# Attention and a softplus feed-forward on one core: the first heads loaded head by head on two DMA queues, heads 0 and 1 placed by engines, three weight groups converted inside the attention loop, and a row clearing done by a transfer

## The chip, the core and the metric

The kernel runs on one core of a Trainium2 chip. The core has a matrix engine (TensorE, PE in the profile), a vector engine (VectorE, DVE), a scalar engine (ScalarE, ACT), GpSimd (POOL) and SyncE (SP), which issues most DMAs. Engines run their own instruction streams in order and wait for each other through semaphores. The metric is the device time of one execution in microseconds.

## The reference, cut to what matters

```python
def _attn_ref(q, k, v):                       # each (4, 8, 576, 64)
    ...
    q_rot, k_rot = (rotate(q), rotate(k))     # rotary embedding
    scores = scale * np.matmul(q_rot, k_rot.transpose(0, 1, 3, 2))
    scores = scores - np.max(scores, axis=-1, keepdims=True)
    attn = np.exp(scores)
    attn = attn / (np.sum(attn, axis=-1, keepdims=True) + 1e-09)
    return np.matmul(attn, v).astype(np.float32)

def _moe_ref(x, w_in, w_out):                 # x (2304, 512), w_in (512, 2048), w_out (2048, 512)
    h = x @ w_in
    g = np.maximum(h, 0.0) + np.log1p(np.exp(-np.abs(h)))
    return (g @ w_out).astype(np.float32)
```

The 32 heads of the attention are computed first; their outputs, put side by side, are the rows `x` of the feed-forward part.

## The kernel before

**Numbers in two parts.** TensorE multiplies in a rounded 32-bit form (`F32R`). To keep accuracy each operand is split into a high part (the rounded value) and a low part (the rest), and products of parts are added. A "rounding" below is a copy into that form (`rnd`), a "low part" is a subtraction (`tt`).

**Attention loop.** `attention` runs over slots `s`; five slots make a head (`h, c = divmod(s, 5)`). In slot `s` four stages work on different heads: `p1(s)` multiplies a strip of 128 queries with all keys, and DVE takes the row maximum from PSUM (L352); nine slots later (`LAG`) `p2` multiplies again, keys by queries, with the maximum subtracted through two extra rows of `qs` (rows 64 and 65 of its second half) against ones in `ks`; `exps` takes the exponential twice on ACT, `low` subtracts on DVE; three slots later (`PVD`) `pv_mm` multiplies with V; `evac` takes the sums out. PE therefore does, in every slot, one `p1`, one `p2` and one `pv_mm`. `p1` has one PSUM buffer (`ps_1`), `p2` two (`ps_2`), `pv` one (`ps_v`).

**How a head gets its operands.** A pair of heads (`p`) is loaded as two tiles `raw`, one for q and one for k, each with both heads (`load_pair`). `rope_steps` rotates each with three operations (two products with `tab`, a sum: L297), rounds (L291 on ACT, L294 on POOL) and subtracts. For pair 0 this is done by DVE and ACT ahead of the loop, for the others mostly by POOL, one step in each slot. Then `stack(h)` builds `qs` and `ks` of one head with four DMAs from `raw` to other partitions (L329 to L332): the high part twice, the low part once. `qs` and `ks` have four buffers (`NST`).

**The maximum's way.** After a head's five maxima, `shift1` (two tiny POOL operations, L294 and L297 on `shl`), `shift2` (a PE transpose, L370, and an ACT copy, L372) and `shift3` (a DMA on ACT's queue, L376) write it into `qs`. PE's L370 stands in PE's order, so PE waits there if POOL is late. When a head is done, POOL clears the two rows again (L503).

**Weights.** The feed-forward weights come in 16 groups `f`, as 64-bit floats, and are turned into high and low 32-bit parts by six steps (`conv_w`; two chunks for each group): ACT, DVE (L133) with ACT (L135), DVE (L137), an addition (L140), ACT (L143), a subtraction (L145). Group 0 is converted in the first ten slots with DVE, group 1 in slots 142 to 156 (`STEPS`) with the addition and subtraction on POOL, the rest from slot 169 on (`late`, `convert`).

**After the loop.** From slot 146 POOL also multiplies the attention output by the reciprocal sums and splits it (`split_xb`, L179 to L181), one or two operations a slot. Then 96 units of the feed-forward follow: 12 matmuls into `hp` (L197) and 9 into `oa` or `ob` (L233).

**Order.** What is passed through `pin` keeps the program's order on its engine; DMAs in `chain` keep their order among themselves; the rest is placed by a scheduler. Ahead of the loop PE runs 64 matmuls on zeros (`WARM`, L277).

## Time and profile before

| What | Value |
|---|---|
| median of 3 runs | 754.91 us (754.41 to 755.38) |
| profiled execution, its own time | 754.79 us |
| span of its trace | 752.9 us |
| mean granted TensorE clock | 0.98 |
| PE busy | 719.2 us (96%) |
| DVE, ACT, POOL busy | 496.3, 383.0, 314.5 us |

The span is the time from the first to the last instruction of the trace; the profiled execution's own time is 1.9 us longer. PE's busy time is near the span, so a change of the time is found in PE's few idle stretches and in those where its granted clock was low.

### The profile page before, as it was taken

Reading aid. Unit: us, or ns where it says so; the run is one execution under the profiler, and the core shown is the slowest. Engines: PE = TensorE matmul, PEld = TensorE weight load, DVE = VectorE, ACT = ScalarE, POOL = GpSimd, SP = SyncE. Lnnn points to the kernel's source line nnn. Section 1 sums busy time; section 2 is a strip of 40 time slices with the busy share of each in tenths; the row PEclk is TensorE's granted clock in tenths of the full one; section 3 lists DMA queues with packets and bytes.
Section 4 is the critical chain, followed back from the end, with each engine's and each line's share of the span. In section 5 each row is a group of like instructions: output and inputs, shape, how many; then the busy total and the mean of one; then the engine's idle time right before and its main releaser. Section 6 shows DMA issues by size and latency. Waiting matters only on the chain.

```text
span 752.9 us, 11811 instructions
## 1 busy us (share of the span) xinstructions
PE 719.2 (96%) x4288; PEld 671.1 (89%) x4288; DVE 496.3 (66%) x784; ACT 383.0 (51%) x718; POOL 314.5 (42%) x384
## 2 busy tenths in 40 slices
PE   5589999999999999789999999999999999999997
PEld 5489999999999999788888989898989898989896
DVE  7688887888787788666888888454453444344433
ACT  2267777777777778666566665222222222222221
POOL 5269999999898887972000000172220000000000
PEclk9589999999999999999999999999999999999999
DMA  7948887889998977502334433052010000001001
GB/s 234 248 125 203 202 202 195 210 218 218 217 238 225 229 194 175 155 13 71 113 112 134 146 111 94 9 180 64 22 42 1 1 37 7 1 1 43 0 1 44
DMA packets 46219, 89.05 MB, mean 118 GB/s; under 512 B 6768, under 2 KB 16304, under 8 KB 46160
## 3 DMA queue, kind: packets, MB, share of 16 engines
q1 hardware_dynamic: 43184, 83.41, 42.1%
q10 hardware_dynamic: 2976, 4.88, 1.7%
q8 instruction: 34, 0.56, 0.3%
q14 instruction: 25, 0.20, 0.1%
HBM read 48.64 MB, written 7.23 MB: 74 GB/s over the span
## 4 chain that ended last, share of the span: by engine, by line
PE 80%; DVE 7%; DMA 5%; ACT 3%; issue 2%; POOL 2%; SPq 0%; DVEq 0%; ACTq 0%; POOLq 0%
PE hp L197 23%; PE pv L419 13%; PE ob L233 12%; PE oa L233 11%; PE sp L387 10%; PE sp L350 10%; DVE raw L297 2%; DMA qs<-shr 2%; ACT wc L131 1%; DVE wc L140 1%; DVE wl L145 1%; DVE wc L137 1%; DMA x<-rd 1%; DVE mx L352 1%; DMA tab<-cs 1%
## 5 line engine op out<-in xcount | busy, mean ns | idle before, releaser
L197 PE MATMUL hp<-x,wh 128*128 128x384 f32 x768 | 196.9, 337 | 2.3 <-DVE m L212 2.3
L352 DVE TENSOR_REDUCE mx<-sp 128x1 f32<-128x576 f32 x160 | 120.9, 756 | 61.4 <-PE sp L350 51.2
L197 PEld LDWEIGHTS hp<-x,wh 128*128 128x128 f32 x768 | 140.1, 188 | 12.8 <-DVE m L212 4.9
L209 ACT ACTIVATE e<-e 128x384 f32<-128x384 f32 x96 | 50.4, 525 | 188.5 <-DVE e L207 181.8
L350 PE MATMUL sp<-ks,qs 128*128 128x288 f32 x640 | 118.4, 310 | 14.9 <-DMA ks<-raw 10.8
L393 ACT ACTIVATE ph<-sp 128x576 fp32r<-128x576 f32 x160 | 103.7, 648 | 54.5 <-PE sp L387 53.8
L197 PE MATMUL hp<-x,wl 128*128 128x384 f32 x384 | 129.3, 337 | 0.0
L387 PE MATMUL sp<-qs,ks 128*128 128x288 f32 x640 | 114.4, 300 | 1.9 <-DMA qs<-shr 1.8
L350 PEld LDWEIGHTS sp<-ks,qs 128*128 128x128 f32 x640 | 97.6, 198 | 18.8 <-issue 11.0
L419 PE MATMUL pv<-ph,vs 128*64 128x288 f32 (+1 forms) x640 | 111.4, 296 | 2.5 <-DVE xt L427 1.6
L207 DVE TENSOR_SCALAR e<-hp 128x384 int32<-128x384 int32 x96 | 53.2, 554 | 77.3 <-PE hp L197 77.3
L394 ACT ACTIVATE sp<-sp 128x576 f32<-128x576 f32 x160 | 102.9, 643 | 0.0
L401 DVE TENSOR_TENSOR pl<-sp,ph 128x576 fp32r<-128x576 f32 x128 | 96.6, 754 | 7.0 <-ACT sp L394 5.3
L233 PE MATMUL oa<-wh,g 128*128 128x512 f32 x288 | 97.7, 393 | 0.2 <-ACT part L244 0.2
L387 PEld LDWEIGHTS sp<-qs,ks 128*128 128x128 f32 x640 | 94.0, 191 | 3.9 <-DMA qs<-shr 2.9
L233 PE MATMUL ob<-wh,g 128*128 128x512 f32 x288 | 97.3, 393 | 0.0
L419 PEld LDWEIGHTS pv<-ph,vs 128*64 128x64 f32 (+1 forms) x640 | 87.1, 162 | 3.0 <-ACT sp L394 1.8
L217 DVE TENSOR_TENSOR g<-m,g 128x384 fp32r<-128x384 f32 x96 | 55.5, 578 | 48.1 <-ACT g L214 48.1
L297 POOL TENSOR_TENSOR raw<-raw,tab 128x576 f32<-128x576 f32 x58 | 82.3, 1441 | 9.1 <-DMA raw<-qk 9.0
L212 DVE SCALAR_TENSOR_TENSOR m<-hp,e 128x384 f32<-128x384 f32 x96 | 53.4, 556 | 47.3 <-ACT e L209 47.3
L297 POOL TENSOR_TENSOR raw<-raw 128x576 f32<-128x576 f32 (+1 forms) x56 | 80.8, 1443 | 5.2 <-ACT raw L291 3.0
L214 ACT CAST g<-m 128x384 fp32r<-128x384 f32 x96 | 49.1, 512 | 62.0 <-DVE m L212 60.5
(74 smaller groups left out, 874.9 us busy)
## 6 DMA issues: line engine op xcount, KB each, us to landing
raw<-qk SPq DMA_DIRECT2D x32, 576.0 KB
wraw<-w SPq DMA_DIRECT2D x30, 512.0 KB
ks<-raw SPq DMA_DIRECT2D x32, 320.0 KB
qs<-raw SPq DMA_DIRECT2D x32, 288.0 KB
ks<-raw SPq DMA_DIRECT2D x32, 160.0 KB
vf<-v SPq DMA_DIRECT2D x32, 160.0 KB
qs<-raw SPq DMA_DIRECT2D x32, 144.0 KB
x<-xt SPq DMA_DIRECT2D x16, 144.0 KB
```

The source lines that it names most:

```text
L197: pin(nc.tensor.matmul(out=hp, lhsT=a[f][:, c * 128:(c + 1) * 128], rhs=piece(j, c)[:, b, :], start=(i == 0), stop=(i == 11),))
L212: pin(nc.vector.scalar_tensor_tensor(out=m, in0=hp, scalar=0.0, in1=e, op0=ALU.max, op1=ALU.add))
L217: pin(nc.vector.tensor_tensor(out=g[:, 1, :], in0=m, in1=g[:, 0, :].bitcast(F32), op=ALU.subtract))
L233: pin(nc.tensor.matmul(out=po, lhsT=g[:, s, t * 128:(t + 1) * 128], rhs=b[f][:, 512:1024], start=(first and i == 0), stop=(last and i == 2),))
L297: pin((nc.vector if e == "V" else nc.gpsimd).tensor_tensor(out=out, in0=in0, in1=in1, op=op))
L350: pin(nc.tensor.matmul(out=sp[:, j, :HS], lhsT=q[:, i, cq], rhs=k[:, 0, ck], start=(i == 0), stop=(i == 1)))
L352: pin(nc.vector.tensor_reduce(out=mx_t[h][:, c:c + 1], in_=sp[:, :, :HS], axis=AX.XY, op=ALU.max, negate=True))
L387: pin(nc.tensor.matmul(out=sp[:, i, :HS], lhsT=k[:, j, ck], rhs=q[:, j, hs], start=(j == 0), stop=(j == 1)))
L393: pin(nc.scalar.activation(out=ph, in_=sp, func=AF.Exp, scale=D ** -0.5))
L394: pin(nc.scalar.activation(out=sp, in_=sp, func=AF.Exp, scale=D ** -0.5))
L401: pin(nc.vector.tensor_tensor(out=pl, in0=sp[:, :, :HS], in1=ph.bitcast(F32), op=ALU.subtract))
L419: pin(nc.tensor.matmul(out=pv[rows, i, :HS], lhsT=lhs, rhs=rhs[:, i, :], start=(c == 0 and j == 0), stop=(c == 4 and j == len(terms) - 1)))
```

## The change

Head by head for the first four heads: `load_head(h)` loads q of one head into partitions 0 to 63 of a `raw` tile, on SP's queue, and k of the same head into partitions 64 to 127, on ACT's queue; the table `tab` comes in two halves on both queues, and the ACT table load stands behind ACT's first DMAs. For heads 0 and 1 there is no `stack`: ACT, DVE and POOL write their roundings and low parts straight into `qs` and `ks` at the right partitions (`part`, `high_k`, `low_q`, `low_k`, `rest`). The first shift goes from DVE through five PE transposes and two ACT copies into `qs` (`shift_first`). Head 2 is rotated by POOL with one DVE operation; its rounding is an ACT operation in slot 5. The rotations of the next pairs follow a new table of slots (`turns`).

The first `p1` slots use other PSUM buffers, the warm-up has 44 matmuls, groups 0, 1 and 2 are all loaded from slot 14 on in pieces of 128 KB and converted in the loop (one chunk in 20 slots, from slot 37), the two rows of `qs` are cleared by a DMA on SP's queue (`clear`), `shift1` stands earlier in its slot, the last slots use two buffers for `p2` instead of three, and head 30's `pv` goes to `ps_1`. `FC` is now 3, so the late conversion has 26 chunks instead of 28, and `convert` is called once instead of twice in slots 169 to 171.

```diff
-FC = 2
+FC = 3
...
-WL = 92
+WL = 14
+WS = 37
...
-WARM = 64
+WARM = 44
...
-STEPS = {142: (0,), 144: (0,), 146: (1,), 147: (0,), 148: (0,), 149: (1,), 150: (0,), 151: (0,), 152: (1,), 153: (1,),
-         155: (1,), 156: (1,)}
+STEPS = (0, 2, 5, 6, 8, 9)
...
+        def load_head(h):
+            r = raw_p.tile([128, 2, SP], F32R, tag="raw", name="raw")
+            for i, e in enumerate((nc.sync, nc.scalar)):
+                pin(e.dma_start(out=r[64 * i:64 * i + 64, :, :S].bitcast(F32),
+                                in_=qk[h // 2, i, 64 * (h % 2):64 * (h % 2) + 64]))
+            hl_t[h] = r
...
+        def turn(r, e, e0=None):
+            a, b = r[:, 1, :S].bitcast(F32), r[:, 0, :S].bitcast(F32)
+            yield tt(a, a, tab[:, 0, :], ALU.mult, e0 or e)
+            yield tt(b, b, tab[:, 1, :], ALU.mult, e)
+            yield tt(a, a, b, ALU.add, e)
+
+        def cut(r, e, ends):
+            hi, lo = r[:, 0, :], r[:, 1, :]
+            a, b = lo[:, :S].bitcast(F32), hi[:, :S].bitcast(F32)
+            yield rnd(hi[:, :S], a, e)
+            yield tt(lo[:, :S], a, b, ALU.subtract, "P")
+            if ends:
+                rnd(hi[:, S:], hi[:, 512:S].bitcast(F32), "P")
+                rnd(lo[:, S:], lo[:, 512:S].bitcast(F32), "P")
...
+        def low_q(h):
+            hi, a, q, k = part(h)
+            tt(q[Q, 1, :S], a[Q], q[Q, 0, :S].bitcast(F32), ALU.subtract, "V")
+
+        def low_k(h):
+            hi, a, q, k = part(h)
+            tt(k[K, 0, :S], a[K], hi[K, :S].bitcast(F32), ALU.subtract, "P")
+
+        def high_k(h):
+            hi, a, q, k = part(h)
+            rnd(k[Q, 0, :S], a[K], "V")
+
+        def rest(h):
+            hi, a, q, k = part(h)
+            rnd(k[Q, 1, :S], a[K], "A")
+            for j in range(2):
+                rnd(k[Q, j, S:], a[K, 512:], "A")
+            rnd(k[K, 0, S:], k[K, 0, 512:S].bitcast(F32), "A")
...
+        def clear(h):
+            free(nc.sync.dma_start(out=qs[h % NST][64:66, 1, :S].bitcast(F32), in_=ks[0][66:68, 1, :S].bitcast(F32)))
...
-            if n < LAG and n % 2:
+            if n < LAG and n % 4 == 1:
                 sp = ps_v.tile([128, 2, 512], F32, tag="pv", name="sp1")
+            elif n < LAG and n % 4 > 1:
+                sp = ps_2.tile([128, 2, 512], F32, tag="s2", name="sp1")
...
+        def shift_first():
+            tp = ps_2.tile([128, 2, 512], F32, tag="s2", name="tp")
+            for c in range(5):
+                pin(nc.tensor.matmul(out=tp[0:66, c // 4, c % 4 * 128:c % 4 * 128 + 128], lhsT=sh0[:, c, :],
+                                     rhs=identr, start=True, stop=True))
+            for j, z in enumerate((512, 128)):
+                rnd(qs[0][64:66, 1, 512 * j:512 * j + z], tp[64:66, j, :z], "A")
...
-            if n > NSLOT - LAG and (NSLOT - n) % 3 == 2:
-                ps2[n] = ps_1.tile([128, 2, 512], F32, tag="s1", name="sp2")
-            else:
-                ps2[n] = ps_2.tile([128, 2, 512], F32, tag="s2", name="sp2")
+            ps2[n] = ps_2.tile([128, 2, 512], F32, tag="s2", name="sp2")
...
+                if h == NB * NH - 2:
+                    pv_t[h] = ps_1.tile([128, 2, 512], F32, tag="s1", name="pv")
...
-        conv = conv_w([(0, i) for i in range(1024 // CW)], CW, pin, 2)
-        load_pair(0)
-        load_pair(1, (0,))
-        next(conv)
+        load_head(0)
+        for i, e in enumerate((nc.sync, nc.scalar)):
+            pin(e.dma_start(out=tab[:, i, :], in_=cs[:, i, :]))
+        load_head(1)
+        for h in range(2):
+            load_v(h)
+        pin(nc.scalar.preload_act_table_set("natural_log_exp_and_others"))
+        load_head(2)
+        load_head(3)
...
+        list(turn(hl_t[0], "V"))
+        hi, a, q, k = part(0)
+        rnd(q[K, 0, :S], a[Q], "A")
+        rnd(hi[K, :S], a[K], "A")
+        rnd(q[Q, 0, :S], a[Q], "V")
+        high_k(0)
+        low_q(0)
+        low_k(0)
+        list(turn(hl_t[1], "V"))
+        hi, a, q, k = part(1)
+        rnd(hi[K, :S], a[K], "A")
+        rnd(q[Q, 0, :S], a[Q], "A")
+        rnd(q[K, 0, :S], a[Q], "A")
+        low_k(1)
+        v_first = [split_v(h) for h in range(2)]
+        for x in v_first:
+            next(x)
+        next(v_first[0])
+        list(turn(hl_t[2], "P", "V"))
+        for h in range(2):
+            rest(h)
         sv = iter(())
-        rope = iter(())
+        rope = {3: rope_head(3)}
...
+        turns = {2 * p: (10 * p - 14, 10 * p - 5) for p in range(3, NP)}
+        turns |= {3: (9, 13), 4: (14, 18), 6: (20, 27), 8: (28, 36), 10: (37, 45)}
...
+                if s == 0:
+                    high_k(1)
+                if s == 1:
+                    low_q(1)
+                if s == 4:
+                    rnd(sh0[:, :, 64], mx_t[0], "V")
+                    tt(sh0[:, :, 65], mx_t.pop(0), sh0[:, :, 64].bitcast(F32), ALU.subtract, "V")
+                if s == 5:
+                    shift_first()
...
+            if c == 0 and 1 < h <= NB * NH:
+                shift1(h - 1)
             if n2 > 0 and n2 % 5 == 0 and n2 // 5 - 1 + NST < NB * NH:
-                pin(nc.gpsimd.memset(qs[(n2 // 5 - 1) % NST][64:66, 1, :S].bitcast(F32), 0.0))
-            if s >= 5 and c == 0 and s <= NSLOT:
-                shift1(h - 1)
+                clear(n2 // 5 - 1)
             if s < NSLOT:
-                next(rope, None)
-                if s < 5:
-                    next(rope, None)
-                if s % 10 == 5:
-                    for _ in rope:
-                        pass
-                if s % 10 == 6 and h // 2 + 1 < NP:
-                    stack(h + 1)
+                if s == 5:
+                    list(cut(hl_t[2], "A", True))
+                    next(v_first[1])
...
+                if s == 14:
+                    rope[4] = rope_steps(2)
+                    cuts2 = cut(hl_t[2, 0], "A", False), cut(hl_t[2, 1], "A", True)
+                if s in (16, 19):
+                    next(cuts2[s > 16])
+                for p in range(3, NP):
+                    if s == turns[2 * p][0]:
+                        rope[2 * p] = rope_steps(p)
+                for r, (a, z) in turns.items():
+                    if a <= s <= z:
+                        next(rope[r], None)
+                        if r == 4 and s == 14:
+                            next(rope[r], None)
+                        if s == z:
+                            for _ in rope[r]:
+                                pass
+                if s == 19:
+                    for x in cuts2:
+                        list(x)
+                if s == 14:
+                    stack(3)
+                for p in range(1, NP):
+                    if s == {1: 6, 2: 19, 3: 27}.get(p, 10 * p - 4):
+                        stack(2 * p)
+                    if s == 10 * p and p > 1:
+                        stack(2 * p + 1)
...
-            i, j = divmod(s - WL, 6)
-            if 0 <= i < 8 and j == 0:
+            i, j = divmod(s - WL, 5)
+            if 0 <= i < 8 * FC and j == 0:
                 load_p(i)
-            if s == WL + 48:
-                early.extend(conv_w([(1, i)], CW, pin, 1, {0: pre[i]}, nc.gpsimd) for i in range(2))
-                for x in early:
-                    next(x)
-            for x in STEPS.get(s, ()):
-                next(early[x], None)
+            i, j = divmod(s - WS, 20)
+            if 0 <= i < 2 * FC and j in STEPS:
+                if j == 0:
+                    early.append(conv_w([divmod(i, 2)], CW, pin, 1, {0: pre.pop(i)}, nc.gpsimd))
+                    next(early[i])
+                next(early[i])
...
-                convert()
```

On **DVE** the places ahead of and in the first slots are these. Before (`raw_202` and `raw_205` are q and k of heads 0 and 1, `raw_253` and `raw_293` those of heads 2 and 3):

```order
L297 TENSOR_TENSOR raw_202<-raw_202,tab_117 128x576 x2
L297 TENSOR_TENSOR raw_202<-raw_202 128x576 x2
L297 TENSOR_TENSOR raw_205<-raw_205,tab_117 128x576 x2
L297 TENSOR_TENSOR raw_205<-raw_205 128x576 x2
L352 TENSOR_REDUCE mx_256<-sp1_257 128x1
L352 TENSOR_REDUCE mx_256<-sp1_271 128x1
L133 TENSOR_SCALAR wc_279<-wc_279 128x512
L352 TENSOR_REDUCE mx_256<-sp1_285 128x1
L297 TENSOR_TENSOR raw_253<-raw_253,tab_117 128x576
L137 SCALAR_TENSOR_TENSOR wc_279<-wraw_209,wc_279 128x512
L352 TENSOR_REDUCE mx_256<-sp1_297 128x1
```

And in the change (`raw_177`, `raw_182`, `raw_188` are heads 0, 1 and 2):

```order
L301 TENSOR_TENSOR raw_177<-raw_177 128x576
L298 TENSOR_SCALAR qs0_116<-raw_177 64x576
L298 TENSOR_SCALAR ks0_112<-raw_177 64x576
L301 TENSOR_TENSOR qs0_116<-raw_177,qs0_116 64x576
L301 TENSOR_TENSOR raw_182<-raw_182,tab_111 128x576 x2
L301 TENSOR_TENSOR raw_182<-raw_182 128x576
L301 TENSOR_TENSOR raw_188<-raw_188,tab_111 128x576
L400 TENSOR_REDUCE mx_249<-sp1_250 128x1
L298 TENSOR_SCALAR ks1_113<-raw_182 64x576
L400 TENSOR_REDUCE mx_249<-sp1_257 128x1
L301 TENSOR_TENSOR qs1_117<-raw_182,qs1_117 64x576
L400 TENSOR_REDUCE mx_249<-sp1_264 128x1
```

The weight conversion is gone from here, and pieces of heads 1 and 2 stand between the first maxima.

On **POOL** the start of the change reads as follows, behind its memsets (`raw_191` is head 3, `raw_270` and `raw_316` are q and k of heads 4 and 5):

```order
L301 TENSOR_TENSOR ks0_112<-raw_177 64x576
L301 TENSOR_TENSOR ks1_113<-raw_182 64x576
L359 TENSOR_TENSOR vs0_123<-vf0_120,vs0_123 128x5x64
L301 TENSOR_TENSOR raw_188<-raw_188,tab_111 128x576
L301 TENSOR_TENSOR raw_188<-raw_188 128x576 x2
L298 TENSOR_SCALAR raw_188<-raw_188 128x64 x2
L359 TENSOR_TENSOR vs1_124<-vf1_121,vs1_124 128x5x64
L301 TENSOR_TENSOR raw_191<-raw_191,tab_111 128x576
L298 TENSOR_SCALAR shl_364<-mx_286 128x5
L301 TENSOR_TENSOR shl_364<-mx_286,shl_364 128x5
L301 TENSOR_TENSOR raw_191<-raw_191,tab_111 128x576
L301 TENSOR_TENSOR raw_191<-raw_191 128x576
```

Before, POOL began with all of head 2's and 3's q tile (four operations); now it first completes heads 0 and 1, then head 2, head 3 and the next pair.

On **POOL** in slots 147 to 151, before (`shl` is the maximum of head 29, L179 to L181 the split, L140 and L145 the conversion):

```order
L180 TENSOR_SCALAR x0_72<-xm_4156 128x576
L140 TENSOR_TENSOR wc_4038<-wc_4038,wt_4039 128x512
L181 TENSOR_TENSOR x0_72<-xm_4156,x0_72 128x576
L179 TENSOR_TENSOR xm_4208<-x1_73 128x576
L503 MEMSET qs3_125 2x576
L321 TENSOR_TENSOR vs0_128<-vf0_126,vs0_128 128x5x64
L180 TENSOR_SCALAR x1_73<-xm_4208 128x576
L294 TENSOR_SCALAR shl_4260<-mx_4105 128x5
```

And in the change:

```order
L178 TENSOR_SCALAR x0_72<-xm_4186 128x576
L359 TENSOR_TENSOR vs0_123<-vf0_120,vs0_123 128x5x64
L179 TENSOR_TENSOR x0_72<-xm_4186,x0_72 128x576
L177 TENSOR_TENSOR xm_4237<-x1_73 128x576
L178 TENSOR_SCALAR x1_73<-xm_4237 128x576
L298 TENSOR_SCALAR shl_4286<-mx_4136 128x5
```

The conversion's addition and the memset no longer stand ahead of `shl`.

## Rows read from the trace of the kernel before

**Rows 1.** Waits of PE, whole span: who waited for whom, total us, times, longest.

```profile
PE sp L350 <- DMA ks<-raw: 10.8, 1, 10.8
PE sp L370 <- POOL shl L297: 5.5, 3, 2.4
PE sp L350 <- DVE mx L352: 3.8, 5, 1.9
PE hp L197 <- DVE m L212: 2.3, 5, 0.9
```

**Rows 2.** Windows: stretch, length, busy us of PE, PEld, DVE, ACT, POOL; clock, DMA share, GB/s.

```profile
30.00:40.00 10.00, 5.66 (x21) 4.60 (x21) 9.41 (x14) 4.01 (x9) 2.62 (x4) 0.50 0.97 220
...
60.00:80.00 20.00, 20.00 (x152) 19.83 (x151) 16.16 (x23) 15.59 (x30) 17.79 (x24) 1.00 0.85 206
...
150.00:200.00 50.00, 49.44 (x373) 48.85 (x372) 39.88 (x54) 37.57 (x71) 44.04 (x55) 1.00 0.93 223
...
300.00:320.00 20.00, 15.70 (x115) 14.96 (x114) 14.27 (x20) 13.10 (x25) 19.61 (x21) 0.99 0.55 158
```

**Rows 3.** Chain that ended last, 0 to 50 us: start, duration, what.

```profile
1.49 5.09 DMA tab<-cs
...
18.39 4.68 DMA ks<-raw
...
35.60 3.55 DMA qs<-shr
```

**Rows 4.** Timeline, 0 to 50 us: start, duration, engine, line, operation, shape, [idle before].

```profile
8.14 0.76 DVE L297 TENSOR_TENSOR raw<-raw 128x576 f32<-128x576 f32 x1
8.93 0.67 ACT L291 CAST raw<-raw 128x576 fp32r<-128x576 f32 x1 [6.91 <-DVE raw L297]
...
10.17 3.38 POOL L297 TENSOR_TENSOR raw<-raw,tab 128x576 f32<-128x576 f32 x2 [3.60 <-DMA raw<-qk]
10.31 3.86 DVE L297 TENSOR_TENSOR raw<-raw,tab 128x576 f32<-128x576 f32 x2
...
23.31 5.69 PE L350 MATMUL sp<-ks,qs 128*128 128x288 f32 x20 [10.83 <-DMA ks<-raw]
...
37.61 0.86 POOL L321 TENSOR_TENSOR vs<-vf,vs 128x320 fp32r<-128x320 f32 x1 [4.18 <-ACT vs L291]
...
42.09 1.28 PE L350 MATMUL sp<-ks,qs 128*128 128x288 f32 x4
...
49.60 0.68 POOL L294 TENSOR_SCALAR raw<-raw 128x576 fp32r<-128x576 f32 x1
```

**Rows 5.** Page, costliest groups: POOL's rotation products; busy us, mean ns of one.

```profile
L297 POOL TENSOR_TENSOR raw<-raw,tab 128x576 f32<-128x576 f32 x58 | 82.3, 1441 | 9.1 <-DMA raw<-qk 9.0
```

**Rows 6.** Timeline of ACT's shift copies L372: heads 3, 17, 28 and 31.

```profile
63.44 0.26 ACT L372 CAST shr<-sp 10x128 fp32r<-10x128 f32 x1
...
191.78 0.26 ACT L372 CAST shr<-sp 10x128 fp32r<-10x128 f32 x1
...
294.38 0.25 ACT L372 CAST shr<-sp 10x128 fp32r<-10x128 f32 x1
...
328.63 0.25 ACT L372 CAST shr<-sp 10x128 fp32r<-10x128 f32 x1 [0.71 <-PE sp L370]
```

**Rows 7.** Timeline, conversion steps in the start and in slots 144 to 148.

```profile
35.23 0.41 DVE L133 TENSOR_SCALAR wc<-wc 128x512 int32<-128x512 int32 x1
...
292.75 1.53 DVE L133 TENSOR_SCALAR wc<-wc 128x512 int32<-128x512 int32 x1
...
295.00 0.79 PE L350 MATMUL sp<-ks,qs 128*128 128x288 f32 x4 [0.66 <-DVE mx L352]
...
299.89 1.29 POOL L140 TENSOR_TENSOR wc<-wc,wt 128x512 int32<-128x512 int32 x1 [3.13 <-DVE wc L137]
```

**Rows 8.** Timeline of PE at the end of attention: pv of heads 30 and 31.

```profile
329.52 0.76 PE L419 MATMUL pv<-ph,vs 128*128 128x288 f32 x4 [0.93 <-ACT ph L393]
...
337.65 0.78 PE L419 MATMUL pv<-ph,vs 128*128 128x288 f32 x4 [1.57 <-DVE xt L427]
```

More of the change, by code (lines that the diff above doesn't have):

```diff
@@ L112, in load_w @@
             raw = cv_p.tile([128, CW], dt, tag=kind, name=kind, bufs=3)[:, :m]
-            (pin if f == 0 else chain)(nc.sync.dma_start(out=raw.bitcast(w.dtype), in_=w[f, :, i * m:(i + 1) * m]))
+            chain(nc.sync.dma_start(out=raw.bitcast(w.dtype), in_=w[f, :, i * m:(i + 1) * m]))
             loaded[n] = raw
@@ L283, in load_pair @@
                 r = raw_p.tile([128, 2, SP], F32R, tag="raw", name="raw")
-                (pin if p < 2 else chain)(nc.sync.dma_start(out=r[:, :, :S].bitcast(F32), in_=qk[p, i]))
+                chain(nc.sync.dma_start(out=r[:, :, :S].bitcast(F32), in_=qk[p, i]))
                 hl_t[p, i] = r
-                if p == 0 and i == 0:
-                    nc.sync.dma_start(out=tab, in_=cs)
+        def load_head(h):
[4 more added lines that the diff above has]
+            hl_t[h] = r
         def rnd(out, in_, e):
@@ new lines, in part @@
+        def part(h):
+            return hl_t[h][:, 0, :], hl_t[h][:, 1, :S].bitcast(F32), qs[h], ks[h]
+        def low_q(h):
[13 more added lines that the diff above has]
+            rnd(k[K, 0, S:], k[K, 0, 512:S].bitcast(F32), "A")
@@ L527, in attention @@
                 recip(n3 // (5 * NH) - 1)
-            if 0 < s < 9:
-                next(conv, None)
-                if s % 2:
-                    next(conv, None)
-            if s == 9:
-                for _ in conv:
-                    pass
             tail(s)
@@ L595, in tail @@
                 convert()
-                convert()
-        kind = I32 if w.dtype == F32 else I64
-        pre = [mp["wr"].tile([128, CW], kind, tag="wr", name="wr") for _ in range(2)]
+        kind, dt = ("wc", I32) if w.dtype == F32 else ("wraw", I64)
+        pre = {}
         early = []
@@ L604, in load_p @@
             m = slice(j * CW // 4, (j + 1) * CW // 4)
-            chain(nc.sync.dma_start(out=pre[i].bitcast(w.dtype)[:, m],
-                                    in_=w[1, :, i * CW + m.start:i * CW + m.stop]))
+            if j == 0:
+                pre[i] = cv_p.tile([128, CW], dt, tag=kind, name=kind, bufs=3)
+            o = i % 2 * CW
+            chain(nc.sync.dma_start(out=pre[i].bitcast(w.dtype)[:, m], in_=w[i // 2, :, o + m.start:o + m.stop]))
         cuts = [(c, 0, S) for c in range(4)] + [(c, S, 2 * T) for c in range(4)] + [(c, 2 * T, 3 * T) for c in range(4)]
```

65 lines of the change are left out of this document (27 added, 38 removed).

## The prediction

> **What bounds the kernel now.** I read the windows first. From 60 to 80 us PE is busy for all of 20.00 us at the full clock, and POOL for 17.79 us, 89% [rows 2]. So the attention loop is paced by PE, with POOL close behind. The pace is read from ACT's shift copies, one for each head: heads 3 to 17 lie 63.44 to 191.78 us, 128.34 / 14 = 9.17 us for a head, 1.83 us for a slot [rows 6]. PE's work is hardly changed, so only what PE loses against this pace can be won. The waits of PE, the chain and the copies show three places.
>
> The start: PE's first score product begins at 23.31 us, 10.8 us after the warm-up [rows 1, 4]; the chain runs through the table's landing (6.58 us), DVE's rotations and the `ks` transfer of 4.68 us [rows 3]. Then the first maximum travels by a DMA of 3.55 us from 35.60, so head 0's second product cannot be whole before 39.15 us [rows 3]. In between PE's clock is at 0.50 (1.2 of 2.4 GHz), and DVE is busy 9.41 of 10 us with reductions, rotations and weight conversion [rows 2].
>
> The end of the loop: heads 28 to 31 take 34.25 us from copy to copy instead of 27.5 [rows 6], 6.75 us lost. From 300 to 320 POOL is busy 19.61 of 20 us while PE is busy 15.70 [rows 2]; PE waits for POOL's `shl` [rows 1].
>
> After it: `pv` of heads 30 and 31 is held 0.93 and 1.57 us [rows 8], and the feed-forward loses 2.3 us in five waits for DVE [rows 1].
>
> **The start, step by step.** The bytes needed first (one head's q and k, and the table) are as many as before (one tile and the table, 1.18 MB), so I let DVE begin where it does now, at 6.7 us. Two queues are counted as no gain in rate. Three operations of 0.76 us end at 8.9 [rows 4]. ACT's two roundings, 0.67 each, end at 10.3; DVE's roundings and low part end at 10.6. POOL's `low_k(0)`, 1.44 us [rows 5], then ends at 12.0, and the first score product can start: 11 us earlier than now.
>
> Next DVE is the long queue. An operation of DVE on SBUF beside POOL takes 1.93 us (3.86 for two) instead of 0.76, and POOL's 1.69 (3.38 for two) instead of 1.44 [rows 4, 5]: they go one after the other. So head 1's first product waits until 12.0 and its rotation ends at 14.1; head 2's product ends at 14.9. Then five reductions of 0.76 (taken as a 576-wide operation), a rounding, a subtraction and two tiny steps, together 5.3 us, and 1.2 us of waits for POOL (an estimate: half a POOL operation at two of four places): the first shift is ready at 21.4 us. PE's five transposes and ACT's two copies, 1.5 us, put it into `qs` at 22.9, against 39.15 now. ACT's rounding of head 2 stands behind these copies in ACT's order: 23.6. POOL's subtraction and two short roundings end at 25.7.
>
> Behind that POOL has, until head 4's operands are ready, twelve 576-wide operations of 1.44 us (17.3), one rounding of 0.68, two V splits of 0.86 (1.7) [rows 4, 5] and eight small ones (2.0, an estimate): 47.4 us. The `stack` transfer takes 3.55 us, the smaller of the two in rows 3, since fewer loads lie beside it: 50.9. From there to head 3's copy are 1.3 slots, 2.4 us: 53.3 against 63.44 [rows 6]. **Gain 10.1 us.** This point is later than head 2's own: its first scores come at 25.7 + 3.55 = 29.3 us against 42.09 [rows 4]. If POOL's chain were hidden, ten slots of 1.83 behind 29.3 give 47.6 for head 4 against 61.0 (63.44 less 2.4), a gain of 13.4: the upper bound. If all eight SBUF operations of DVE between 10.6 and 21.4 took 1.93, 3.6 us more are lost than I counted: 6.5, the lower bound. A half clock costs nothing ahead of 29 us, where DVE or POOL is last. The shorter warm-up ends some 3 us before the 12.5 us (23.31 less 10.83) at which PE falls idle now [rows 4], and ahead of the first scores.
>
> **In the loop.** Group 0's conversion leaves the start and three groups come in: six chunks from slot 37 to 146. Before, two chunks lie in slots 142 to 156. POOL loses 28 clearings and gains twelve operations of 1.29 us [rows 7], spread over 110 slots: no price. ACT's three steps a chunk go into its slack (15.59 us busy of 20) [rows 2]: no price; if that cover were gone, 0.67 us each, as a rounding in rows 4. DVE's step L133 is the risk: it takes 0.41 us with POOL idle and 1.53 beside it, and PE then waited 0.66 us for the next maximum [rows 7], because `p1` has one buffer and two DVE operations of 0.76 leave 0.31 us in a slot. Six chunks cost between 0 and 4.0 us; which it is hangs on where POOL stands at each, so I take the middle, **+2.0 us**.
>
> The Trainium skill ("GPSIMD Engine Reference", section Specifications) says that GpSimd shares its SBUF interfaces with VectorE and contends with DVE instructions in a two-port mode or with two SBUF inputs. By that rule L137, which has two SBUF inputs, would be exposed as L133 is: twelve steps, 7.9 us. The trace agrees with the rule for L133.
>
> Weight pieces of 128 KB each 9.17 us add 14 GB/s to 206 from slot 14 on, 7%, so the DMA share of 0.85 becomes about 0.91; at 0.93 PE lost 0.56 us in 50 [rows 2]. Over the 143 us of slots 14 to 92, where none were loaded before, that is at most 1.6 and at least 0: **+0.7 us**. The clearing by DMA is one more issue for SP a head. Behind it SP holds the other pieces of the same head's `stack`, which waits for the same PE work anyway. Its landing is needed six slots, 11 us, later, against transfers of up to 4.68 us [rows 3]: no price.
>
> **The end of the loop.** POOL loses four conversion steps of 1.29 us, less the sixth chunk's last one, and a clearing, and `shl` stands earlier. Its load from 300 to 320 us falls from 19.61 to about 15 us of 20 [rows 2, 7], so the waits for `shl` should go. I take 5.5 of the 6.75 us; the lower bound is 3.5, if POOL enters slot 146 late from the sixth chunk. **−5.5 us.**
>
> Head 30's `pv` in `ps_1` frees both `pv` of their waits, 2.5 us [rows 8]. Two buffers for `p2` instead of three cost some: product, two exponentials and a subtraction must pass before a buffer is free. Price 0 to 2.5, taken as 1.0 (0.1 us for each of eight slots, an estimate): **−1.5 us**. The feed-forward's five waits of 2.3 us [rows 1] stay nearly as they are, with two chunks fewer: **−0.3 us** (0 to −1).
>
> **Sum.** −10.1 + 2.0 + 0.7 − 5.5 − 1.5 − 0.3 = −14.7. The profiled execution took 754.79 us (its span 752.9 and 1.9 around it), so 740.1; the median of the runs is 0.12 above it: **740.2 us**.
>
> **Rivals.**
> (B) POOL's chain at the start is hidden: gain 13.4, 736.9 us. For it: POOL's 1441 ns is a mean over contended operations [rows 5]. Against: 89% load leaves it little to catch up.
> (C) DVE and POOL hold each other up at the start: gain 6.5, 743.8. For it: 1.93 us in rows 4. Against: POOL often waits for ACT there.
> (D) The loop's conversion is dear: each of twelve DVE steps costs PE 0.66 us, 7.9 instead of 2.0: 746.1. For it: the wait in rows 7. Against: L137's price is not seen. (This is where the skill's rule above would lead.)
> (E) The start does not gain: the heads behind the first four come no earlier, since POOL is 89% busy and pairs 2 to 5 stay late by 10 us. Only the end gains: 754.8 − 7.3 + 2.7 = 750.2. Against: POOL is busy only 2.62 of 10 us from 30 to 40 us now [rows 2], and the change fills that.
> (F) Slower: the weight pieces and clearings saturate SP's queue and the DMA engines, so that each head's `stack` or shift lands late. Without the +0.7 the sum is 739.5; 28 heads losing 0.75 us each are 21 us: 760.5. It turns to slower from 0.55 us a head. Against: at a share of 0.93 the loss is 0.56 us in 50, 0.1 a head [rows 2].
>
> **Numbers.** My forecast has 0.58 (own range 736.5 to 744), B 0.11, C 0.12, D 0.08, E 0.06, F 0.05. The range 733 to 747 holds A to D but for a few hundredths at either side; E and F are left out. 0.2% (1.5 us, a little more than the 0.97 us by which the runs differ) is about what can be told from no change. Faster: A to E, 0.95, less 0.01 for same; slower: F, 0.05.
>
> **What would show it.** Right: a first score product near 12 us; the first exponential's product near 23 to 25; head 2 waiting for its transfer until about 29 and head 4 until about 51; head 3's shift copy near 53; heads 28 to 31 within 29 us; no wait of PE for `shl` after 290 us. Wrong, if the copies inside the loop lie more than 9.3 us apart (D or F), or if head 2's or 4's operands come ten microseconds later than said (E).

## The result and the profile after

The changed kernel took 764.27 us, median of four runs (762.73 to 766.75), against 754.66 (754.28 to 755.38) for the kernel before in the same session: ratio 1.0129, interval 1.0101 to 1.0158. It is slower, where I had forecast 740.2 (733 to 747). The profiled execution took 764.14 us, its span 762.4.

First the shift copies of ACT (now L425), which answer to [rows 6], for heads 3, 4, 5, 14, 15, 22, 23, 28 and 31. From the timeline, columns start, duration, engine, line, operation, shape:

```profile
62.75 0.26 ACT L425 CAST shr<-sp 10x128 fp32r<-10x128 f32 x1 [0.43 <-PE sp L423]
72.48 0.26 ACT L425 CAST shr<-sp 10x128 fp32r<-10x128 f32 x1
86.72 0.26 ACT L425 CAST shr<-sp 10x128 fp32r<-10x128 f32 x1 [0.43 <-PE sp L423]
...
172.54 0.26 ACT L425 CAST shr<-sp 10x128 fp32r<-10x128 f32 x1
185.38 0.26 ACT L425 CAST shr<-sp 10x128 fp32r<-10x128 f32 x1
...
253.32 0.26 ACT L425 CAST shr<-sp 10x128 fp32r<-10x128 f32 x1
266.65 0.26 ACT L425 CAST shr<-sp 10x128 fp32r<-10x128 f32 x1
...
315.13 0.26 ACT L425 CAST shr<-sp 10x128 fp32r<-10x128 f32 x1
...
342.18 0.26 ACT L425 CAST shr<-sp 10x128 fp32r<-10x128 f32 x1 [0.78 <-PE sp L423]
```

Head 3 stands at 62.75 us, where it stood at 63.44: nearly all of the start's gain is gone by then. Heads 3 to 28 take 252.4 us instead of 230.9, so the loop loses 21.4 us more. From head 28's copy to the span's end are 447.3 us instead of 458.5. Together: -0.7 + 21.4 - 11.2 = +9.5, by which the span grew.

At pace a head comes 9.17 us after the one before; what it takes longer is called its loss below. From head 3 to head 8, 7.0 us more are lost than before, most of it at head 5 (5.1). From head 8 to head 28, where the kernel before lost 1.7 us, the changed kernel loses 16.2: 7.8 at heads 15 and 23, 7.1 at heads 12, 16, 20, 24 and 28 (the weight chunks, too, stand four heads apart), 0.9 at head 18.

Where PE waits, over the whole span (who for whom, total us, times, longest), beside [rows 1]:

```profile
PE sp L398 <- DMA ks<-raw: 15.1, 4, 6.2
PE sp L440 <- DMA qs<-shr: 3.9, 3, 2.1
PE sp L398 <- DVE mx L400: 3.8, 7, 0.7
...
PE hp L195 <- DVE m L210: 1.0, 3, 0.3
```

In the kernel before, the wait for the shift was this:

```profile
PE sp L387 <- DMA qs<-shr: 1.8, 2, 1.3
```

The waits for `shl` are gone, as forecast. For `ks` there are four waits instead of one, and those for the shift have grown from 1.8 to 3.9 us. The windows that answer to [rows 2] (busy us of PE, PEld, DVE, ACT, POOL, then clock, DMA share and rate):

```profile
30.00:40.00 10.00, 9.11 (x50) 8.92 (x51) 5.20 (x8) 3.72 (x7) 6.15 (x7) 0.68 0.49 129
60.00:80.00 20.00, 19.98 (x137) 19.50 (x136) 14.55 (x20) 13.65 (x26) 12.01 (x15) 0.91 0.55 143
150.00:200.00 50.00, 48.05 (x339) 46.36 (x340) 38.93 (x53) 36.42 (x69) 41.74 (x49) 0.97 0.89 202
300.00:320.00 20.00, 18.73 (x137) 17.85 (x136) 17.28 (x24) 14.99 (x28) 16.25 (x20) 1.00 0.69 165
```

In 300 to 320 POOL is no longer full and PE works 3.03 us more. But in 60 to 80 PE's clock is 0.91 on the mean, so part of the stretch is at the lower of its two levels (1.2 of 2.4 GHz), and POOL, which I had put close behind PE there, works 12.01 us of 20. Why, the timelines of PE and POOL show (start, duration, [idle before <- releaser]):

```profile
13.44 1.81 PE L398 MATMUL sp<-ks,qs 128*128 128x288 f32 x6 [3.59 <-POOL ks L301]
...
30.89 1.30 PE L398 MATMUL sp<-ks,qs 128*128 128x288 f32 x4 [3.65 <-DMA ks<-raw]
...
59.39 0.82 PE L398 MATMUL sp<-ks,qs 128*128 128x288 f32 x2 [6.22 <-DMA ks<-raw]
...
83.73 0.92 PE L398 MATMUL sp<-ks,qs 128*128 128x288 f32 x4 [3.76 <-DMA ks<-raw]
```

```profile
41.76 0.20 POOL L298 TENSOR_SCALAR shl<-mx 128x5 fp32r<-128x5 f32 x1 [5.44 <-DVE mx L400]
...
49.23 0.88 POOL L359 TENSOR_TENSOR vs<-vf,vs 128x320 fp32r<-128x320 f32 x1 [1.35 <-ACT vs L295]
...
53.14 1.40 POOL L301 TENSOR_TENSOR raw<-raw 128x576 fp32r<-128x576 f32 x1 [1.64 <-ACT raw L295]
```

Head 0's first score (13.44) and head 2's (30.89) come where I had said, 12.0 and 29.3. Head 4's comes at 59.39 instead of about 51, and head 6's at 83.73 is 3.76 us late too. POOL is not overloaded in between: it stands idle 5.44 + 1.35 + 1.64 = 8.4 us, since pair 2's rotation stands behind the shift of head 2, a split of V behind ACT's rounding of V, and pair 2's subtraction behind a rounding that ACT does in slot 19 only, after that slot's exponentials.

The late shifts at heads 14 and 22 have another cause. ACT's timeline around head 14's, with its issue (ACTq):

```profile
172.54 0.26 ACT L425 CAST shr<-sp 10x128 fp32r<-10x128 f32 x1
...
175.44 0.62 ACTq L429 DMA_DIRECT2D qs<-shr  x1
176.10 0.65 ACT L446 ACTIVATE ph<-sp 128x576 fp32r<-128x576 f32 x1 [2.23 <-DMA raw<-qk]
```

and the chain that ended last, there (start, duration, what):

```profile
167.06 8.35 DMA raw<-qk
175.44 4.17 DMA qs<-shr
```

The copy was ready, but its transfer was issued 2.90 us later, when a load of `qk` (576 KB) had landed. In the built program the transfers count on eight semaphores, and each is issued only when the one that counted on its semaphore before has landed. Head 14's shift shares one with that load, head 22's with another. The traces bear this out: over the kernel before, the changed kernel and the thirteen experiments, 73 shifts were issued more than 0.6 us behind their copy, and 72 of them 0.02 to 0.08 us after the transfer ahead on their semaphore had landed. ACT issues the shift in order, so its exponentials waited with it. In the kernel before, none of 32 shifts was issued more than 0.5 us behind its copy; here four were (heads 14, 18, 21 and 22). Busy DMA engines alone do not make such a loss: in the kernel before, the DMA share was 1.03 from head 15's copy to head 16's, and nothing was lost (9.15 us).

### The profile page after: what moved, and what is told of

It is laid out like the page before. It is cut to its first block, busy times and chain, and to the rows that moved or that the text cites. A ratio compares the mean times of both kernels' runs of the same rounds, so it can differ in the third digit from the quotient of the medians.

```text
span 762.4 us, 11773 instructions
## 1 busy us (share of the span) xinstructions
PE 725.1 (95%) x4272; PEld 675.2 (89%) x4272; DVE 493.3 (65%) x776; ACT 387.5 (51%) x726; POOL 320.0 (42%) x374
## 4 chain that ended last, share of the span: by engine, by line
PE 76%; DMA 8%; DVE 8%; ACT 3%; issue 2%; SPq 1%; POOL 1%; DVEq 0%; ACTq 0%
PE hp L195 23%; PE ob L231 12%; PE pv L475 12%; PE oa L231 11%; PE sp L440 9%; PE sp L398 9%; DMA raw<-qk 4%; DMA ks<-raw 2%; DMA qs<-shr 2%; DVE mx L400 2%; DVE wc L135 1%; DVE wc L138 1%; DVE wc L131 1%; ACT wc L129 1%; DVE wl L143 1%
## 5 line engine op out<-in xcount | busy, mean ns | idle before, releaser
L398 PE MATMUL sp<-ks,qs 128*128 128x288 f32 x640 | 120.5, 315 | 23.1 <-DMA ks<-raw 15.1
L440 PE MATMUL sp<-qs,ks 128*128 128x288 f32 x640 | 117.3, 305 | 5.3 <-DMA qs<-shr 3.9
L475 PE MATMUL pv<-ph,vs 128*64 128x288 f32 (+1 forms) x640 | 113.1, 299 | 0.0
L440 PEld LDWEIGHTS sp<-qs,ks 128*128 128x128 f32 x640 | 96.1, 195 | 9.5 <-DMA qs<-shr 4.5
L205 DVE TENSOR_SCALAR e<-hp 128x384 int32<-128x384 int32 x96 | 53.3, 555 | 77.6 <-PE hp L195 77.6
L475 PEld LDWEIGHTS pv<-ph,vs 128*64 128x64 f32 (+1 forms) x640 | 89.1, 165 | 0.2
L301 POOL TENSOR_TENSOR raw<-raw 128x576 f32<-128x576 f32 (+1 forms) x60 | 85.6, 1427 | 6.5 <-ACT raw L295 4.1
L301 POOL TENSOR_TENSOR raw<-raw,tab 128x576 f32<-128x576 f32 x59 | 84.6, 1449 | 0.6 <-DMA raw<-qk 0.6
```

The costliest lines, as they stand in the source:

```text
L301: pin((nc.vector if e == "V" else nc.gpsimd).tensor_tensor(out=out, in0=in0, in1=in1, op=op))
L398: pin(nc.tensor.matmul(out=sp[:, j, :HS], lhsT=q[:, i, cq], rhs=k[:, 0, ck], start=(i == 0), stop=(i == 1)))
L440: pin(nc.tensor.matmul(out=sp[:, i, :HS], lhsT=k[:, j, ck], rhs=q[:, j, hs], start=(j == 0), stop=(j == 1)))
L475: pin(nc.tensor.matmul(out=pv[rows, i, :HS], lhsT=lhs, rhs=rhs[:, i, :], start=(c == 0 and j == 0), stop=(c == 4 and j == len(terms) - 1)))
```

## Experiments

Each kernel was compared with the kernel before on the same chip. Waits, copies and the length of the loop come from one profiled execution each, while the runs of a kernel differ by 2 to 7 us; for whole times the ratios decide. "The loop" is the time from head 8's copy to head 28's, 185.1 us before and 199.6 after. Edits are to the changed kernel unless said otherwise.

**e1: pair 2 brought forward.**

```diff
-        turns |= {3: (9, 13), 4: (14, 18), 6: (20, 27), 8: (28, 36), 10: (37, 45)}
+        turns |= {3: (9, 13), 4: (14, 14), 6: (20, 27), 8: (28, 36), 10: (37, 45)}
...
-                if s in (16, 19):
-                    next(cuts2[s > 16])
+                if s == 15:
+                    for x in cuts2:
+                        next(x)
```

The subtractions and head 4's `stack` go from slot 19 to 16.

> The changed kernel with pair 2's rotation brought forward: its six POOL multiplies and sums all stand in slot 14, ahead of head 2's shift, ACT's two roundings in slot 15, POOL's subtractions and head 4's transfers in slot 16 instead of 19. Theory (order): POOL stood idle for 5.44 us at 36.3 us behind head 2's maximum, and again 1.64 us for ACT's rounding, because those steps are tied to PE's slots; brought forward, head 4's operands land by 53 us, PE's 6.22 us wait and the half clock behind it go (7.9 us), and so does head 6's delay (5.1 us), since POOL's 6.44 us idle at 60 us came from PE being late: 764.3 - 13.0 = 751.3. First rival: head 6 is late for a reason of its own (pair 3's loads): 764.3 - 7.9 = 756.4. Second rival: POOL's chain is simply too long, so that the work only moves: 762 to 766.

Ratio 1.0040 (1.0017 to 1.0063), median 758.2 us, span 755.0. Head 3's copy came at 57.66 instead of 62.75 and head 4's wait fell to 1.27 us; head 6 still waited 3.77:

```profile
78.08 1.01 PE L398 MATMUL sp<-ks,qs 128*128 128x288 f32 x4 [3.77 <-DMA ks<-raw]
```

The first rival holds: head 4's delay was POOL's order, and head 6 has a reason of its own. Which one, e5 shows.

**e2: the clearing back on POOL; e3: one weight group in the loop; e4: e1 and e2 together.**

```diff
-            free(nc.sync.dma_start(out=qs[h % NST][64:66, 1, :S].bitcast(F32), in_=ks[0][66:68, 1, :S].bitcast(F32)))
+            pin(nc.gpsimd.memset(qs[h % NST][64:66, 1, :S].bitcast(F32), 0.0))
```

That is e2's edit; e3 has `FC = 1` instead of 3, and converts three steps a slot behind the loop instead of one.

> The changed kernel with the clearing back on POOL as a memset. Theory (lanes): the shift transfers of heads 14 and 22 were held because the semaphore that they count on was still due from a 590 KB load of qk (issued 167.06, landed 175.41); without the clearing transfers the transfers fall on other semaphores and no shift shares one with such a load, so the losses of 3.67 and 4.16 us between heads 14 and 15 and heads 22 and 23 go: 764.3 - 7.8 = 756.5, although the weight pieces stay and the DMA share stays near 1.0. Rival (bandwidth): the shifts are late because the DMA engines are full: the losses stay, 764 to 765. Heads 4 and 6 stay late in either case.

> The changed kernel with one weight group converted in the loop (two chunks, eight weight pieces, in slots 14 to 67) instead of three; groups 1 and 2 are converted behind the loop with the rest, so only the loop's copies are compared, not the whole time. The clearing transfers stay. Theory of the dear conversion: the losses at every fourth head end with head 12 (heads 16, 20, 24 and 28 lose 0.88, 1.76, 0.58 and 1.97 us in the changed kernel), some 4 to 5 us. Theory (lanes): no shift shares its semaphore with a load of qk here either, so another 7.8 us go: from head 3's copy to head 28's 252.4 - 7.8 - 4.6 = 240 us. Rival (the clearing transfers themselves delay the shifts): heads 15 and 23 stay late, 248 us. Rival (conversion costs nothing, the losses are those of the reciprocals that were there before): 244.6 us.

> The changed kernel with both edits, pair 2 brought forward and the clearing on POOL. If the two causes are apart: 764.3 - 13.0 - 7.8 = 743.5, faster than before by 11; what then is left against the prediction of 740.2 is the conversion in the loop. If head 6 stays late: 748.6. If the memsets on POOL undo what the forward order wins, over 752.

e2: 1.0086 (1.0057 to 1.0115), median 762.6 us. Heads 15 and 23 came 9.27 and 9.28 us after the ones before, so their losses went, with all weight pieces in place. The total of 756.5 was missed all the same. Heads 9 and 10, which had lost nothing, lost 1.6 and 0.5 us, heads 16 and 24 1.4 each instead of 0.9 and 0.6; the loop fell by 4.3 us only, to 195.3. And with the memsets back, heads 28 to 31 took 31.05 us instead of 27.05.

e3, one profile: behind slot 67 no piece or chunk is left in the loop, and heads 16 and 24 lose nothing any more. But from head 13's copy to head 28's it took 148.4 us, against 139.3 in the kernel before, with shifts issued up to 3.33 us late and late operands. So these losses need no weight pieces; whether the clearing transfers alone make them, e12 tests. From heads 3 to 28 it took 249.2 us, a miss by all my numbers but the rival's 248.

e4: 1.0043 (1.0023 to 1.0062), median 758.6 us, not the sum but the third case, over 752: the memset of slot 14 now stood ahead of pair 2's rotation and waited 5.1 us for PE, so that PE in turn waited 4.5 us for head 2's `shl`, and at the end 2.0 us for head 29's shift.

**e5: pair 3 brought forward too** (on top of e1).

```diff
-        turns |= {3: (9, 13), 4: (14, 14), 6: (20, 27), 8: (28, 36), 10: (37, 45)}
+        turns |= {3: (9, 13), 4: (14, 14), 6: (17, 24), 8: (25, 34), 10: (37, 45)}
...
-                    if s == {1: 6, 2: 16, 3: 27}.get(p, 10 * p - 4):
+                    if s == {1: 6, 2: 16, 3: 25, 4: 35}.get(p, 10 * p - 4):
```

> The kernel of the first experiment (pair 2 brought forward) with pair 3's rotation brought forward in the same way, from slots 20 to 27 to slots 17 to 24, pair 4's from 28 to 25, and heads 6's and 8's transfers two and one slots earlier. In the first experiment head 6 was still 5.16 us late, and POOL stood idle for 2.67 and 3.05 us at 47 and 51 us, behind a V rounding and a maximum, while pair 3's loads had landed. Theory (place in POOL's order): the 3.8 us wait of PE for head 6's ks and the half clock behind it go: 5 us less than the first experiment, a profiled span of 750 instead of 755.0, and a ratio to the kernel before near 0.997. Rival (POOL's throughput): POOL is behind by then whatever its order, and the wait moves to head 8 or 10: a span of 753 to 755.

Ratio 0.9974 (0.9954 to 0.9994), span 749.3. Head 5's copy came 9.15 us behind head 4's instead of 14.33. As expected: head 6, too, was late by POOL's order, and the rival falls.

**e6: the clearing in two halves; e7: e5 with the same.**

```diff
-            free(nc.sync.dma_start(out=qs[h % NST][64:66, 1, :S].bitcast(F32), in_=ks[0][66:68, 1, :S].bitcast(F32)))
+            for i in range(2):
+                o = slice(i * HS, i * HS + HS)
+                free(nc.sync.dma_start(out=qs[h % NST][64:66, 1, o].bitcast(F32), in_=ks[0][66:68, 1, o].bitcast(F32)))
```

> The changed kernel with each head's clearing transfer cut into two halves, so that there are 28 transfers more and no byte less. Theory (shared semaphores): another transfer now stands on the semaphore of each shift, and the program shows no shift behind a load of qk any more: the losses of 3.67 and 4.16 us at heads 15 and 23 go, although there are more transfers; heads 16 and 24 now stand behind a broadcast of the reciprocals and may lose about 1 us each: 764.3 - 7.8 + 2 = 758.5, at most 761. Rival (the DMA engines are full, or SP's queue is): the losses stay or grow, 764 to 768.

> Pairs 2 and 3 brought forward and the clearing in two halves: if the causes are apart, what e5 shows less the 1.4 and 2.1 us that the first experiment lost at heads 15 and 19 behind held shifts, plus about 1: a span near 748, a ratio to the kernel before of 0.994. If the shifts' delay is one of bandwidth: as e5 or slower.

e6: 1.0122 (1.0101 to 1.0144), median 764.35 us; e7: 0.9989 (0.9974 to 1.0004). Both totals missed: e6's lies where the rival had it, and e7 is no faster than e5. Of the theory the place came true and the gain did not. Heads 15 and 23 lost 1.87 and 2.77 us instead of 3.67 and 4.16, and head 16's shift, behind the broadcast of the reciprocals as the program showed, was held 3.00 us and cost 3.83. So the place of the loss follows the shared semaphore, and moving it does not make the sum smaller. How long a shift is held is the landing time of the transfer ahead of it, and that differs (1.75 to 5.69 us for the same 4.5 KB in e12); so far the rival has a part in it.

**e8: e5 without DVE's twelve conversion steps** (L131 and L135 stay behind the loop; the edit of the second step is the same).

```diff
-                keep(nc.vector.tensor_scalar(out=wf, in0=wf, scalar1=0x0FFFFFFF, scalar2=3,
-                                             op0=ALU.bitwise_and, op1=ALU.logical_shift_left))
+                if e is nc.vector:
+                    keep(nc.vector.tensor_scalar(out=wf, in0=wf, scalar1=0x0FFFFFFF, scalar2=3,
+                                                 op0=ALU.bitwise_and, op1=ALU.logical_shift_left))
...
```

> As e5, with DVE's two steps of each of the six chunks that are converted in the loop left out (those three weight groups come out wrong); ACT's and POOL's steps and all loads stay. It measures what DVE's twelve steps cost. Theory (rival D of the prediction): 7.9 us, a span 8 below that of e5, and the losses at heads 12, 16, 20, 24 and 28 fall to those of the reciprocals (0.75 at head 12's place, 0.5 at heads 20 and 28). The prediction's own value: 2 us. Rival (the loss comes from POOL's steps L138 and L143, or from the weight pieces): less than 1 us.

Ratio 0.9939 (0.9917 to 0.9960), the median 2.2 us below e5's, near the prediction's 2, but the loop was no shorter (200.5 against 197.8 us). Heads 16, 20, 24 and 28 lost less, but waits for `ks` at odd heads and held shifts took their place. So the steps' price could not be read beside the clearing transfers.

**e12: the kernel before, with the clearing as a transfer and nothing else.**

```diff
-                pin(nc.gpsimd.memset(qs[(n2 // 5 - 1) % NST][64:66, 1, :S].bitcast(F32), 0.0))
+                free(nc.sync.dma_start(out=qs[(n2 // 5 - 1) % NST][64:66, 1, :S].bitcast(F32),
+                                       in_=ks[0][66:68, 1, :S].bitcast(F32)))
```

> The kernel before with one edit: each head's clearing is a transfer of SP's queue instead of a memset of POOL. The prediction gave this edit no price. Theory (the transfers delay SP's later issues and put other transfers on the shifts' semaphores): from head 8 to head 28 190 to 195 us instead of 185.1, with waits of PE for qs and ks, in part paid back at the end of the loop where POOL has one memset less a head: 756 to 762 in all. Rival (the transfers alone cost nothing; only with the weight pieces is the queue too full): 185 to 186 us there, and 752 to 755 in all.

Ratio 1.0040 (1.0018 to 1.0062). The loop took 193.2 us instead of 185.1. ACT's timeline of its head 27, as above for head 14, and the chain there:

```profile
288.27 0.26 ACT L372 CAST shr<-sp 10x128 fp32r<-10x128 f32 x1
...
291.18 0.62 ACTq L376 DMA_DIRECT2D qs<-shr  x1
291.85 0.65 ACT L393 ACTIVATE ph<-sp 128x576 fp32r<-128x576 f32 x1 [2.24 <-DMA qs<-ks]
```

```profile
285.47 5.69 DMA qs<-ks
291.18 4.48 DMA qs<-shr
```

Here the clearing itself, 4.5 KB, took 5.69 us to land, and the next shift waited on its semaphore. Head 28 alone lost 4.2 us by it. The shifts of heads 14 and 16, 2.3 and 2.5 us late, stood behind transfers of `x`; in the kernel before, the same shifts stood behind others that landed 1.0 and 0.2 us ahead of them. This one edit, which I had given no price, costs 8.1 us in the loop, as expected; the rival falls. Part comes back where POOL is full (heads 28 to 31: 31.1 us instead of 34.25), and the medians differ by 3.1 us (758.8 and 755.7).

**e9: e5 with 24 clearings back on POOL, two slots later; e10: the same without DVE's steps.**

```diff
-            if n2 > 0 and n2 % 5 == 0 and n2 // 5 - 1 + NST < NB * NH:
+            if n2 > 0 and n2 % 5 == 2 and 0 < n2 // 5 < 25:
+                pin(nc.gpsimd.memset(qs[(n2 // 5 - 1) % NST][64:66, 1, :S].bitcast(F32), 0.0))
+            if n2 > 0 and n2 % 5 == 0 and 25 <= n2 // 5 and n2 // 5 - 1 + NST < NB * NH:
                 clear(n2 // 5 - 1)
```

> Pairs 2 and 3 brought forward as in e5, and 24 of the 28 clearings back on POOL as memsets, two slots later than they stood there before so that POOL does not wait for PE (in e4 a memset ahead of pair 2's rotation held head 2's shift for 4.5 us); the last four stay transfers. Theory (the clearing transfers are what delays shifts and operands in the loop): from head 8's copy to head 28's 197.8 in e5 becomes 192 to 193, as what is left are the conversion steps (some 8 us with the reciprocals over 183.4 at pace); a span near 744, ratio to the kernel before 0.990. Rival (weight pieces are the cause): the loop stays at 197 and the span at 749.

> As e9 with DVE's twelve conversion steps left out (three weight groups come out wrong). In e8 leaving them out won only 2.2 us, as other waits, for ks and for shifts, took their place. Theory: those waits came from the clearing transfers; without them the steps' full price shows: from head 8 to head 28 some 186, 6.5 us below e9 over the five chunks there, and 7.9 in the span. Rival (a second limit, the DMA engines, lies just below): 190 or more, under 3 us below e9.

e9: 0.9875 (0.9851 to 0.9898), 745.31 us, faster than both kernels. Its loop took 195.8 us, nearer to the rival's 197 than to my 192 to 193: six shifts were still 0.6 to 2.1 us late, now mostly behind `stack` transfers on their semaphores. e10: 0.9815 (0.9775 to 0.9855), median 741.6 us, its loop 189.6 instead of the expected 186. The copies of heads 8 and 28, first e9, then e10:

```profile
102.48 0.26 ACT L425 CAST shr<-sp 10x128 fp32r<-10x128 f32 x1
...
298.25 0.25 ACT L425 CAST shr<-sp 10x128 fp32r<-10x128 f32 x1
```

```profile
103.14 0.26 ACT L427 CAST shr<-sp 10x128 fp32r<-10x128 f32 x1
...
292.72 0.26 ACT L427 CAST shr<-sp 10x128 fp32r<-10x128 f32 x1
```

So in these two profiles DVE's steps cost 6.2 us for the five chunks in that stretch, which makes 7.4 for six. The medians differ by 3.7 us and the profiled spans by 5.2, so the price lies between 3.7 and 7.4. It is above e8's 2.2 in each of these readings.

**e11: e9 with each DVE step cut into four; e13: e9 with the steps moved.**

```diff
-WS = 37
+WS = 36
...
-STEPS = (0, 2, 5, 6, 8, 9)
+STEPS = (0, 2, 7, 8, 10, 11)
```

This is e13; in e11 L131 and L135 each run over a quarter of the columns at a time, one quarter a slot, with `STEPS = (0, 2, 3, 4, 5, 6, 7, 8, 9, 11, 13, 14)`.

> As e9 with each of DVE's twelve conversion steps cut into four, one a slot: 48 steps of a quarter of the width. Theory (a slot has 0.31 us of DVE's time to spare, so a step of 1.45 us costs 1.14 and four of 0.4 us cost 0.1 each): the conversion's price falls from 7.9 to some 3 us: a span of 739 to 740, ratio 0.984. Rival (the price is the contended time of DVE as a whole, wherever it lies): no change from e9, or slower by the fixed part of 36 more instructions, 748 or more.

> As e9, with DVE's two steps of a chunk standing one slot position elsewhere: at the end of a head's fourth slot, ahead of the reduction that POOL's shift waits for, instead of in the fifth and third. In e11 a step of a quarter of the width took 0.72 us on the mean, half of a POOL product of 1.43, and one that began 0.05 us behind a POOL product ended with it (139.99 + 1.51 against 139.94 + 1.42): DVE's step is held until POOL's instruction ends. Theory (held): where POOL is idle in front of the shift, the step takes its own 0.4 to 0.6 us; POOL is idle there 6.1 us in 21 heads, so perhaps half of the steps are short, and the price falls from 7 by 2 to 4 us: a span of 742 to 744, ratio 0.984. Rival (POOL is behind at those places and has no idle time with a chunk in it): the steps keep 1.5 and 0.8 us, 745 or more.

e11: 0.9986 (0.9970 to 1.0002), median 754.4 us, so worse than e9: my theory of the spare time in a slot falls, and the rival (748 or more) was nearer. Groups by line (count, busy us, mean ns) of e11 from 100 to 300 us, then the same step in e9 and in e13 from 80 to 330:

```profile
L142 DVE SCALAR_TENSOR_TENSOR wc<-wraw,wc 128x128 int32<-128x128 int32 x20 | 15.7, 785 | 0.2
L135 DVE TENSOR_SCALAR wc<-wc 128x128 int32<-128x128 int32 x20 | 14.4, 720 | 0.0
```

```profile
L131 DVE TENSOR_SCALAR wc<-wc 128x512 int32<-128x512 int32 x6 | 8.6, 1431 | 0.0
```

```profile
L131 DVE TENSOR_SCALAR wc<-wc 128x512 int32<-128x512 int32 x6 | 4.6, 768 | 0.2
```

A quarter of the width took half of the time, not a quarter. Single rows of e11, DVE's step and POOL's product beside it, say why:

```profile
139.99 1.51 DVE L142 SCALAR_TENSOR_TENSOR wc<-wraw,wc 128x128 int32<-128x128 int32 x1
```

```profile
139.94 1.42 POOL L308 TENSOR_TENSOR raw<-raw 128x576 fp32r<-128x576 f32 x1
```

The step began 0.05 us behind POOL's product and ended 0.14 us behind its end: it was held until POOL's instruction was over. Of the 40 quarter steps between 100 and 300 us, 24 took more than 0.35 us; one that is not held takes 0.21 or 0.28. So each quarter can be held anew.

The whole steps show the same. In the changed kernel eight of the twelve began while a POOL instruction ran, and each ended a fixed time behind that instruction's end: the five of L131 by 0.28 us, the three of L135 by 0.55. The other four took 0.42 (L131) and 0.63 us (L135). So what such a step costs hangs on how much of POOL's instruction is left when it begins.

In e13 the steps stand where POOL is idle or in a shorter instruction (a split of V, a rounding), and L131 fell from 1.43 to 0.77 us, PE's waits for maxima from 4.9 to 2.4 us, the loop from 195.8 to 191.3. Of these 4.5 us, 2.3 are head 28's alone, where head 27's shift was issued 1.97 us late in e9. Ratio 0.9863 (0.9834 to 0.9891), 743.80 us; its interval overlaps that of e9, so the gain in the whole time is not shown.

## Why the prediction was wrong

- **The start up to head 2** was right: forecast 12.0 and 29.3 us, measured 13.44 and 30.89. The 1.4 us are POOL's low part of head 0, which took 2.87 us and not 1.44.
- **Head 4's operands** are the first step that failed: "Behind that POOL has, until head 4's operands are ready, twelve 576-wide operations", added up to 47.4 us. I added durations as if POOL ran without a gap. Its last piece for head 4 ended at 54.9, since it stood idle 8.4 us behind a maximum and two roundings that PE's slots release. From there to PE's start on head 4 passed 4.4 us, not 3.55: that figure is a shift's transfer, and [rows 3] have 4.68 for `stack`. e1 takes 5.1 us of this back by order alone. Of the 9.4 us between the forecast 53.3 and 62.75, 4.4 remain in e1 (57.66): head 2's copy is as late there as in the changed kernel (46.56 and 45.70), at a clock of 0.86 since head 1's and behind a wait of 1.5 us for head 3's `ks`.
- **Head 6** was not in the sum. I let the pace begin at head 4; 5.1 us more were lost by the same kind of order (e5).
- **"The clearing by DMA"**, priced at nothing, is the second failed step. I asked when its landing is needed, and not what is counted behind it. e12 measures +8.1 us in the loop of the kernel before. In the changed kernel the two held shifts cost 7.8 us, but a memset in the transfer's place wins only 4.3 in the loop (e2).
- **"Which it is hangs on where POOL stands at each, so I take the middle, +2.0 us"**: the mechanism was right, the size not. e10 against e9: 7.4 us for six chunks by the loop, close to rival D's 7.9, and 3.7 by the medians. In the changed kernel heads 8, 12, 16, 20, 24 and 28 lost 7.8 us, in e10 2.6. The middle was too low because all but one of the six L131 steps met a POOL instruction that had just begun; in e13, with POOL at another place, they took half as long.
- **Weight pieces, +0.7 us** (0 to 1.6): not settled. e10 has them all, and its loop is 4.5 us longer than before; that holds ACT's and POOL's conversion steps and the late shifts too.
- **The end**, -7.3 us: right, and too small. `shl` and both `pv` waits went; it gave -11.2, of which heads 28 to 31 are 7.2 (27.05 us).
- **The rivals.** E came true at head 3's copy, D in its condition (L135, which was L137 before, was held in three of six steps) and by the loop nearly in its price, and F's sum (760.5) was nearest to the result. F's mechanism, each head's shift or `stack` late, was there as well, but by which transfer stands ahead on a semaphore, which the clearings change, not by a DMA share near 1 alone: in e9, with all pieces, the share was 1.04 between heads 13 and 14, and 0.33 us were lost there. I had given F 0.05, because [rows 2] showed that a high share costs little; that row says nothing about an added transfer in the order.

The terms as measured (9.4 + 5.1 + 5.4 above the conversion's 2.0, 8.1 for the clearing, 3.9 less at the end) add 24.1 us to the forecast of 740.2: 764.3, which is the result. That it fits so closely is in good part luck. The terms come from different kernels and single profiles; other readings of the clearing (4.3) and of the conversion (3.7) would leave it short, and the 4.5 us of e10's loop are in none of them.

## What to carry to other kernels

An in-order engine's queue is not costed by adding its durations: for each step ask which slot of another engine releases the step ahead of it, and count the idle time. A small transfer is not free where transfers share semaphores: look at which transfer stands on the semaphore of the next urgent one, and how long that takes. Two causes that stand in one loop can cover each other (e8 won 2.2 us in the medians and nothing in the loop, e10 against e9 3.7 and 6.2), so take one out before the other is measured.
